# Which piece of SBUF comes next: slots of a backward pass chosen by megabytes stored since their return

## The chip, the core and the metric

The kernel runs on one core of one Trainium2 chip. The metric is the device time of one launch, in microseconds, as the median of several runs. One further execution is recorded by the hardware profiler, and its views are read below. Engine names are those of the profile: PE is the matrix engine, DVE the vector engine, ACT the scalar engine, POOL the GpSimd engine, SP the sync engine that here issues nearly all DMAs. MB are millions of bytes; a transfer that is called 1 MB or 2 MB in the code's terms has 1024 or 2048 KB.

## The reference

One decode step of an attention block with a cache and of a gated feed-forward block, forward and backward, in bfloat16. B = 4 rows, one query each, D = 512, H = 32 heads, a cache of Sk = 4096 positions, Dh = 128, F = 1792.

```python
q = (layernorm(x) @ wq) split into 32 heads            # [4, 32, 1, 128]
p = softmax(q . k_cache / sqrt(128))                   # k_cache, v_cache: [4, 32, 4096, 128]
h = x + (p . v_cache) @ wo
out = h + (silu(layernorm(h) @ w1) * (layernorm(h) @ w3)) @ w2
# outputs: out, and the gradients of sum(out * grad_out)
# for x, k_cache, v_cache, wq, wo, w1, w3, w2
```

With one query per head, the gradients of the two caches are outer products: for v_cache it is p (4096 long) times the gradient of the head's output (128 long), for k_cache it is the gradient of the scores times q. Each is as large as the cache itself. So the kernel must read both caches (2 x 134 MB), read v_cache once more in the backward pass for the gradient of p, and write two gradients of 134 MB each. The other gradients are small: out_4 (wq) and out_5 (wo) have 4.2 MB each, out_6, out_7, out_8 (w1, w3, w2) 1.8 MB each.

## The kernel before

The unit of work is one of 128 pairs (row, head), here called a head: 1 MB of k_cache and 1 MB of v_cache. The forward pass loads K and V of each head (lines 168 and 176 of the code). A middle part computes the feed-forward block and the gradients that lead to each head's output. The backward pass then goes over the heads again: the first SP = 32 one at a time (V loaded at L823, V gradient stored at L807, K gradient at L1234), the other 96 as NT = 48 pairs of heads. For a pair:

- `load_pair` (L1259) loads the two V of the pair with one 2 MB transfer,
- `front_pair` transposes them on PE (L1276), copies the result back over the same slots on ACT (L1277) and multiplies with dO, the gradient of the head's output (L1291); after that the V data are no longer needed,
- `grad_pair` takes two slots, fills them with an outer product on DVE (`outer_pair`, L1357) and stores them with one 2 MB transfer (L1367). It is called for out_3 (V gradient) by `more_V` and for out_2 (K gradient) in the loop over pairs.

DVE's outer products read p doubled by POOL (`P2_pair`, L1354, from rows that `P_rows` puts into the tile Pp by four matmuls and an ACT copy, L1329 and L1331) and rows of dO or q repeated over the partitions (`replicate_pair`, eight matmuls L1344 and an ACT cast L1347, once for four pairs and each of dO and q).

Beside the pairs runs `side_work`, a generator that is advanced by two yields at each call of `side`, four per pair. In this order it computes the gradient of x, the four 1 MB pieces of the gradient of wq (stored to out_4, L1057), loads w2 again (L528), makes row buffers rows1 and rows2 (a POOL DMA L1066, PE transposes L1074, ACT copies L1076), finishes the forward output (PE L1086, DVE L1091), and computes the gradients of w2 (L1101), w1 and w3 (L1117) and wo (L1128).

All data of this size live in one SBUF tensor, `arena`, of NSLOT = 23 slots of about 1 MB. `free` is a queue of free slots. A slot is returned to it in program order, at the moment the instructions that use it are written down, not when they are done: if its last use is a store, the next writer of the slot has to wait on the chip until the store has landed. Before the change a `Slot` takes the one that was returned first; names listed in `SIDE` take the first that lies outside `part["pairs"]`, the eight pairs of adjacent slots (0 to 5 and 8 to 17) that `Slot2` draws from, once `part["B"]` is set (from head 20 of the single heads on). `Slot2` takes the adjacent pair whose later half was returned first. So the lone slots are 6 and 18 to 22; slot 7 is in use throughout.

The order of all work is written out by hand in the loops, each engine executes its instructions in that order, and all large transfers go through SP's one queue, 530 of them. A transfer there also waits for the eighth one before it. Each is cut into sixteen parts, one per DMA engine, and each part leaves a record when it lands.

Of the kernel before, what the change touches and what calls it, by code (L numbers as in the profile page):

```python
# [18 lines left out]
NSLOT = 23  # L19
JQ = 8  # L20
NPE = 1
SP = 32
NPAIR = 8


@with_exitstack
def kernel(
# [25 lines left out]
    B = A_x.shape[0]  # L53
# [9 lines left out]
    DC = D // P  # L63
# [43 lines left out]

    free = deque(range(NSLOT))
    part = {"B": False, "side_done": False}
    SIDE = ("Pp", "wq2", "dqflat", "fin", "rows1", "rows2", "oflat", "w2a", "w2b", "gwq", "gw2", "gw13", "gwo")  # L110
    arena = slotp.tile([P, NSLOT * SLOT], BF16, name="arena")

    class Slot:
        def __init__(self, name, src=free):
            if name in SIDE and part["B"]:
                self.i = next(i for i in free if i not in part["pairs"])
                free.remove(self.i)
            else:
                self.i = src.popleft()
            self.t = arena[:, self.i * SLOT:(self.i + 1) * SLOT]  # L120

        def b(self, n=4096):
# [6 lines left out]
            return self.t[:, 0:SJ * Dh].rearrange("p (j d) -> p j d", d=Dh)  # L129

        def give(self):
            free.append(self.i)

    class Slot2:
        @staticmethod
        def choices():
            at = {i: n for n, i in enumerate(free)}
            return [(max(at[i], at[i + 1]), i) for i in (range(0, NSLOT - 1, 2) if part["side_done"] else sorted(part["pairs"])[::2])
                    if i in at and i + 1 in at]

        def __init__(self):
            self.i = min(self.choices())[1]
# [2 lines left out]
            self.t = arena[:, self.i * SLOT:(self.i + 2) * SLOT]  # L145

        def give(self):
            free.append(self.i)
            free.append(self.i + 1)


    rows_t = pers.tile([32 + B, D], FP32, name="rows_t")
# [45 lines left out]
    for i in range(2):  # L198
        t = fcon.tile([P, 64], BF16, name=f"onesw{i}")
# [132 lines left out]
    def zq_window(z, m):  # L332
        a = 66 * (m % 2) + 32 + (m % 2) - m
        return z[:, a:a + 32]
# [443 lines left out]
    REP = B  # L778
    reps = {}
    V2s, VTs = {}, {}  # L780
# [34 lines left out]
    NV2 = 7  # L815
    vring = deque()
    nv = {"next": 0}
# [137 lines left out]
    with ExitStack() as c2:  # L955
# [44 lines left out]
        def side_work():  # L1000
# [4 lines left out]
            t = rs.f(2080)[:, 1536:1536 + NH]  # L1005
# [6 lines left out]
            flat = Slot("dqflat")  # L1012
# [7 lines left out]
            for cc in range(DC):  # L1020
                wq2 = wq2s.popleft()
# [17 lines left out]
            fs = Slot("fin")  # L1039
# [10 lines left out]
            for cc in range(DC):  # L1050
                st = Slot("gwq")
                for n8 in range(HD // 512):
                    grad_unit(st.b(HD)[:, n8 * 512:(n8 + 1) * 512], xhat_bf[0:B, cc * P:(cc + 1) * P],
                              flat.b(HD)[0:B, n8 * 512:(n8 + 1) * 512])
                    yield
                grad_flush()
                nc.sync.dma_start(out=out_4[cc * P:(cc + 1) * P, :], in_=st.b(HD))  # L1057
                st.give()
            flat.give()
            fs.give()  # L1060
            w2 = load_w2()

            r1, r2 = Slot("rows1"), Slot("rows2")
# [40 lines left out]
            oflat = Slot("oflat")  # L1104
# [49 lines left out]
        def replicate(nm_, i0):  # L1154
            if i0 >= NH or (nm_, i0 // REP) in reps:
                return
            K_ = 8 * B if i0 < 8 * B else P
            rows = dOrows_bf if nm_ == "rdo" else qrows_bf
            ps = psrep.tile([P, REP, Dh], FP32, tag="rep", name="rep_ps")
            for i in range(REP):  # L1160
                nc.tensor.matmul(ps[:, i, :], lhsT=ident_b[0:K_, i0 + i:i0 + i + 1].to_broadcast([K_, P]), rhs=rows[0:K_, :],
                                 start=True, stop=True)
            rt = rep_bufs[nm_][i0 // REP % 2]
            nc.scalar.copy(out=rt, in_=ps[:])
            reps[nm_, i0 // REP] = rt
# [28 lines left out]
        def front(s):  # L1194
            hl = s % B
            if s not in VTs:
                for g in range(SJ // GW):
                    V_T(s, psT, range(g, g + 1))
                    if hl == 0 and g == 0:
                        rows_out()  # L1200
                    if hl == 0 and g == 2:
                        rows_T()
            VT = VTs[s].heads()
            if hl == 0:
                rows["acc"] = psD.tile([P, 512], FP32, tag="dP", name="dP_ps")
            dO_window(s + 2)
            for u in range(2):
                for c in range(4):
                    j0 = 8 * c + 4 * u
                    nc.tensor.matmul(rows["acc"][32 * c:32 * (c + 1), :], lhsT=zq_window(zd[hl], 2 * hl + u),  # L1210
                                     rhs=VT[:, j0:j0 + 4, :], start=(hl == 0 and u == 0),
                                     stop=(hl == B - 1 and u == 1), tile_position=(0, 32 * c))
            if hl == B - 1:
                rows["ps"] = rows.pop("acc")
            sl = VTs.pop(s)
            (vring if nv["next"] < SP and len(V2s) + len(VTs) + len(vring) < NV2 else free).append(sl.i)

        def group_dS(g):
            i0 = g * B
# [22 lines left out]
        NT = (NH - SP) // 2  # L1242
        H0 = SP // B
        pV, pP2, pdS, psl = {}, {}, {}, {}
        npv = {"next": 0}
# [13 lines left out]
            nc.sync.dma_start(out=pV[t].t[:, 0:2 * SJ * Dh], in_=two_heads(A_v_cache, t))  # L1259

        def load_pairs(t):
            while npv["next"] < NT and (npv["next"] <= t or len(V2s) + 2 * len(pV) < 6 and len(Slot2.choices()) > 1):
                load_pair()

        def dO_pair(t):
# [4 lines left out]
        def front_pair(t, mid):  # L1270
            pl = t % 2
            v = pV[t].t[:, 0:2 * SJ * Dh].rearrange("p (j d) -> p j d", d=Dh)
            for g in range(2 * SJ // GW):
                pt = psT.tile([P, GW, P], BF16, tag="tps", name="pt_tps")
                for i in range(GW):
                    nc.tensor.transpose(pt[:, i, :], v[:, g * GW + i, :], ident_b[:])  # L1276
                nc.scalar.copy(out=v[:, g * GW:(g + 1) * GW, :], in_=pt[:])  # L1277
                if pl == 0 and g == 0:
                    rows_out()
                if pl == 0 and g == 2:  # L1280
                    rows_T()
                if g == 3:
                    mid()
            if pl == 0:
                rows["acc"] = psD.tile([P, 512], FP32, tag="dP", name="dP_ps")
            dO_pair(t + 2)
            for u in range(4):
                m = 8 * pl + 2 * u
                for c in range(4):
                    j0 = 16 * c + 4 * u  # L1290
                    nc.tensor.matmul(rows["acc"][32 * c:32 * (c + 1), :], lhsT=zt[t % B][:, 32 - m:64 - m], rhs=v[:, j0:j0 + 4, :],  # L1291
                                     start=(pl == 0 and u == 0), stop=(pl == 1 and u == 3), tile_position=(0, 32 * c))
            if pl == 1:
                rows["ps"] = rows.pop("acc")
            pV.pop(t).give()

        def group_dS_pair(g):
            T = rows.pop("T").rearrange("p jj (c z l u a) -> p z l a c u jj", c=4, z=2, l=2, u=4, a=2)
# [11 lines left out]
        Pp, zt, P2b = {}, [], []  # L1310
# [23 lines left out]
        def replicate_pair(nm_, q):  # L1334
            if q >= NT // B or (nm_, "p", q) in reps:
                return
            s = SP + q * 2 * B
            K_ = 8 * B if s + 2 * B <= 8 * B else P
            rws = dOrows_bf if nm_ == "rdo" else qrows_bf
            ps = psrep.tile([P, REP, Dh], FP32, tag="rep", name="rep_ps")  # L1340
            for i in range(REP):
                for a in range(2):
                    n = s + i + a * B
                    nc.tensor.matmul(ps[64 * a:64 * (a + 1), i, :], lhsT=ident_b[0:K_, n:n + 1].to_broadcast([K_, P // 2]),  # L1344
                                     rhs=rws[0:K_, :], start=True, stop=True, tile_position=(0, 64 * a))
            rt = rep_bufs[nm_][(H0 + q) % 2]
            nc.scalar.copy(out=rt, in_=ps[:])  # L1347
            reps[nm_, "p", q] = rt
# [24 lines left out]
        def more_V(upto):  # L1373
            while gvd["n"] < min(SP, upto):
                s = gvd["n"]
                P_pairs(s)
                replicate("rdo", s - s % REP)
                grad_V(s)
                P_pairs(s + 1)
                P_pairs(s + 2)  # L1380
                gvd["n"] += 1
                if s % REP == 2 and s + 2 < SP:
                    replicate("rdo", s + 2)
                if s >= SP - 2:
                    P2_pair(s - SP + 2)
            while gvd["t"] < NT and SP + 2 * gvd["t"] + 2 <= upto:
                t = gvd["t"]
                P2_pair(t)
                replicate_pair("rdo", t // B)
                grad_pair(out_3, t, pP2.pop(t), reps["rdo", "p", t // B][:, t % B, :])  # L1390
                P2_pair(t + 1)
                gvd["t"] += 1
                if t % B == 2:
                    replicate_pair("rdo", t // B + 1)
# [57 lines left out]
        for t in range(NT):  # L1452
            s = SP + 2 * t
# [46 lines left out]
```

## Time and profile before

| | |
|---|---|
| median of 4 runs | 1697.9 us (1697.28 to 1698.45) |
| the profiled execution | 1698.45 us, of which the span of its instructions is 1696.7 us |
| bytes moved | 707.45 MB, mean 417 GB/s (read 422.59 MB, written 282.34 MB) |
| busy share of the span | PE 73%, DVE 73%, ACT 57%, POOL 20% |
| granted TensorE clock, mean | 0.857 |
| 2 MB stores (x96), issue to landing | 27.9 us |
| 2 MB V loads (x48), issue to landing | 32.1 us |
| where SP's queue waits longest in total | L1367 for DVE's outer products: 587.4 us in 94 waits |

The share of an engine is its busy time over the span. "DMA share" in a window is the mean busy share of the sixteen DMA engines, so one engine of sixteen that is busy alone gives 0.06. The number after an arrow in brackets is how long the engine was idle before the instruction, and on what it waited.

### The profile page before, as it was taken

What the parts mean: (1) busy time and instruction counts of PE and PEld (TensorE: products, weight loads), DVE (VectorE), ACT (ScalarE), POOL (GpSimd) and SP (SyncE); (2) the same over time, 40 slices, a digit from 0 to 9 for tenths busy, and PEclk for the clock granted to TensorE, in tenths of its full rate; (3) what the DMA queues carried; (4) which work ended last, traced back from release to release, by engine and by line L of the source; (5) the groups of instructions that cost most, each with busy time, mean ns of one, the idle gap of its engine ahead of it and who ended that gap; (6) DMA issues with size and microseconds to landing.
All of it is one profiled execution on the core that took longest, in us unless ns stands there. A gap on an engine that the chain in (4) does not pass through costs nothing. (4 is left out here: it accounts for less than half of the span.)

```text
span 1696.7 us, 37845 instructions
## 1 busy us (share of the span) xinstructions
PE 1237.8 (73%) x16228; PEld 950.2 (56%) x16228; DVE 1234.5 (73%) x1198; ACT 959.5 (57%) x1490; POOL 346.4 (20%) x583
## 2 busy tenths in 40 slices
PE   5889888888888888878877665666727766667552
PEld 4777766666677676656655544544425444444331
DVE  5989999999999987667764676575636665565582
ACT  3555454554455444677666566666628766566551
POOL 1211223222222222223331211021004100111000
PEclk9999999999999999799799679867659776676775
DMA  9999999999999999999999999999997999999997
GB/s 401 424 425 423 424 424 425 424 424 424 414 422 414 423 401 399 394 410 425 425 427 426 416 428 429 430 429 428 430 425 307 419 426 426 429 429 430 430 430 341
DMA packets 81000, 707.45 MB, mean 417 GB/s; under 512 B 8748, under 2 KB 12984, under 8 KB 15296
## 3 DMA queue, kind: packets, MB, share of 16 engines
q1 hardware_dynamic: 80416, 704.94, 99.0%
q8 instruction: 127, 2.08, 0.5%
q14 instruction: 41, 0.34, 0.0%
q0 software_dynamic: 416, 0.10, 0.0%
HBM read 422.59 MB, written 282.34 MB: 415 GB/s over the span
## 5 line engine op out<-in xcount | busy, mean ns | idle before, releaser
L1277 ACT COPY arena<-pt_tps 128x1024 bf16<-128x1024 bf16 x384 | 369.3, 1023 | 211.0 <-PE pt_tps L1276 210.6
L1276 PE MATMUL pt_tps<-ident_b,arena 128*128 128x128 bf16 x3072 | 307.0, 272 | 210.4 <-DMA arena<-in_A_v_cache_dram 128.4
L1276 PEld LDWEIGHTS <-arena 128*128 128x128 bf16 x3072 | 264.3, 126 | 311.5 <-issue 155.5
L1357 DVE TENSOR_TENSOR arena<-arena 128x8192 bf16<-128x8192 bf16 x48 | 212.3, 4424 | 255.9 <-DMA out_dram<-arena 224.1
L462 PE MATMUL M_ps<-arena 128*128 128x130 bf16 x4096 | 286.5, 222 | 38.3 <-DMA arena<-in_A_v_cache_dram 38.1
L447 DVE TENSOR_TENSOR arena<-arena 128x4096 bf16<-128x4096 bf16 x128 | 292.4, 2285 | 24.9 <-POOL arena L443 24.9
L462 PEld LDWEIGHTS <-arena 128*128 128x128 bf16 x4096 | 253.8, 99 | 58.9 <-DMA arena<-in_A_v_cache_dram 51.2
L354 DVE STREAM_TRANSPOSE arena<-arena 128x512 f32<-128x512 f32 (+1 forms) x321 | 250.6, 797 | 0.0
L349 ACT COPY arena<-pt_tps 128x1024 bf16<-128x1024 bf16 x128 | 129.4, 1012 | 186.7 <-PE pt_tps L348 147.7
L1357 DVE TENSOR_TENSOR arena<-dS,arena 128x8192 bf16<-128x8192 bf16 x48 | 212.3, 4425 | 19.8 <-DMA out_dram<-arena 19.6
L1354 POOL COPY arena<-arena 128x128 bf16<-128x128 bf16 x48 | 43.7, 911 | 496.7 <-ACT arena L1331 275.9
L360 POOL TENSOR_TENSOR W<-qrep,wmask 128x128 bf16<-128x128 bf16 x128 | 121.3, 948 | 84.9 <-PE S_ps L380 70.1
L791 ACT COPY arena<-pt_tps 128x1024 bf16<-128x1024 bf16 x128 | 122.1, 1024 | 29.0 <-PE pt_tps L790 27.1
L443 POOL COPY arena<-P_all 128x64 bf16<-128x64 bf16 x128 | 32.7, 255 | 413.5 <-ACT P_all L437 410.5
L790 PE MATMUL pt_tps<-ident_b,arena 128*128 128x128 bf16 x1024 | 83.4, 238 | 24.5 <-ACT arena L791 24.2
L790 PEld LDWEIGHTS <-arena 128*128 128x128 bf16 x1024 | 72.0, 109 | 35.2 <-issue 33.7
L1291 PE MATMUL dP_ps<-arena 128*32 128x512 bf16 x768 | 82.6, 454 | 10.4 <-ACT arena L1277 10.2
L796 DVE TENSOR_TENSOR arena<-P,arena 128x4096 bf16<-128x4096 bf16 x29 | 66.4, 2296 | 23.0 <-DMA out_dram<-arena 22.9
L437 ACT COPY P_all<-pt_P 32x64 bf16<-32x64 bf16 x256 | 52.1, 203 | 55.0 <-PE pt_P L433 52.7
L348 PE MATMUL pt_tps<-ident_b,arena 128*128 128x128 bf16 x1024 | 80.5, 223 | 0.0
L796 DVE TENSOR_TENSOR arena<-dS,arena 128x4096 bf16<-128x4096 bf16 x32 | 73.5, 2302 | 7.9 <-DMA out_dram<-arena 7.5
L472 PE MATMUL kP_ps<-arena,onesw 128*32 128x512 bf16 x1024 | 79.2, 386 | 0.0
(245 smaller groups left out, 1600.9 us busy)
## 6 DMA issues: line engine op xcount, KB each, us to landing
out_dram<-arena SPq DMA_DIRECT2D x96, 2048.0 KB, 27.9
arena<-in_A_v_cache_dram SPq DMA_DIRECT2D x160, 1024.0 KB, 15.8
arena<-in_A_k_cache_dram SPq DMA_DIRECT2D x128, 1024.0 KB, 15.4
arena<-in_A_v_cache_dram SPq DMA_DIRECT2D x48, 2048.0 KB, 32.1
out_dram<-arena SPq DMA_DIRECT2D x72, 1024.0 KB, 20.1
arena<-in_A_wq_dram SPq DMA_DIRECT2D x8, 1024.0 KB, 16.0
arena<-in_B_w_dram SPq DMA_DIRECT2D x8, 896.0 KB, 15.0
out_dram<-arena SPq DMA_DIRECT2D x6, 896.0 KB, 28.9
```

The lines of the kernel that those rows point to most:

```text
L349: nc.scalar.copy(out=KT[:, c * GW:(c + 1) * GW, :], in_=pt[:])
L354: nc.vector.transpose(out=KT[:, c * w_:(c + n) * w_], in_=Kn[:, c * w_:(c + n) * w_])
L360: nc.gpsimd.tensor_tensor(out=W[:, hl], in0=qrep[:, :, s:s + 1].to_broadcast([P, 4, 32]), in1=wmask[:, hl, None, :].to_broadcast([P, 4, 32 ...
L447: nc.vector.tensor_tensor(out=PK[:, :, 0:Dh].rearrange("p j (r t) -> p j r t", t=2), in0=Ks[s].heads().rearrange("p j (r t) -> p j r t", t=2),
L462: nc.tensor.matmul(hold["M"][:], lhsT=Vn[:, j, :], rhs=PK[:, j, :], start=(j == 0), stop=(j == SJ - 1))
L790: nc.tensor.transpose(pt[:, i, :], v[:, g * GW + i, :], ident_b[:])
L791: nc.scalar.copy(out=v[:, g * GW:(g + 1) * GW, :], in_=pt[:])
L796: nc.vector.tensor_tensor(out=dst.rearrange("p j (r t) -> p j r t", t=2), in0=col2[:, :, None, :].to_broadcast([P, SJ, Dh // 2, 2]), in1=r ...
L1276: nc.tensor.transpose(pt[:, i, :], v[:, g * GW + i, :], ident_b[:])
L1277: nc.scalar.copy(out=v[:, g * GW:(g + 1) * GW, :], in_=pt[:])
L1291: nc.tensor.matmul(rows["acc"][32 * c:32 * (c + 1), :], lhsT=zt[t % B][:, 32 - m:64 - m], rhs=v[:, j0:j0 + 4, :], start=(pl == 0 and u == ...
L1357: nc.vector.tensor_tensor(out=dst.rearrange("p (j r t) -> p j r t", r=Dh // 2, t=2), in0=col2[:, :, None, :].to_broadcast([P, 2 * SJ, Dh / ...
```

## The change

The slots of the backward pass are chosen by age instead of by their place in the queue. The age of a free slot is the number of slots with a store that were returned since its own return; a slot whose last use was not a store (a V slot after its transposes) counts as OLD = 9 at once. Side work takes the lone slot of greatest age. Other single slots take a lone slot if its age is 9 or more, else the oldest of all. `Slot2` takes the pair whose younger half is oldest. A V pair is loaded ahead only if the oldest free pair has an age of 9 or more. The two buffers flat and fs of the side work (slots of dqflat and fin) are returned just before the last slot of the wq gradient, not after it, and "lnb" becomes a name of the side work. The repeated dO rows of the first four pairs are made during head 30 of the single heads instead of at the first pair.

```diff
+OLD = 9
...
+    given = {"n": 0}
+
+    def age(i):
+        return given["n"] - given.get(i, -NSLOT)
+
+    def gave(*slots, stored=True):
+        given["n"] += len(slots) if stored else 0
+        for i in slots:
+            given[i] = given["n"] - (0 if stored else OLD)
+            free.append(i)
...
         def __init__(self, name, src=free):
-            if name in SIDE and part["B"]:
-                self.i = next(i for i in free if i not in part["pairs"])
-                free.remove(self.i)
-            else:
-                self.i = src.popleft()
+            self.i = src[0]
+            if part["B"] and src is free:
+                lone = sorted((i for i in free if i not in part["pairs"]), key=age, reverse=True)
+                self.i = lone[0] if name in SIDE or lone and age(lone[0]) >= OLD else max(free, key=age)
+            src.remove(self.i)
...
         def give(self):
-            free.append(self.i)
+            gave(self.i)
...
         def choices():
-            at = {i: n for n, i in enumerate(free)}
-            return [(max(at[i], at[i + 1]), i) for i in (range(0, NSLOT - 1, 2) if part["side_done"] else sorted(part["pairs"])[::2])
-                    if i in at and i + 1 in at]
+            return [(-min(age(i), age(i + 1)), i) for i in (range(0, NSLOT - 1, 2) if part["side_done"] else sorted(part["pairs"])[::2])
+                    if i in free and i + 1 in free]
...
                 nc.sync.dma_start(out=out_4[cc * P:(cc + 1) * P, :], in_=st.b(HD))
+                if cc == DC - 1:
+                    flat.give()
+                    fs.give()
                 st.give()
-            flat.give()
-            fs.give()
...
-            (vring if nv["next"] < SP and len(V2s) + len(VTs) + len(vring) < NV2 else free).append(sl.i)
+            if nv["next"] < SP and len(V2s) + len(VTs) + len(vring) < NV2:
+                vring.append(sl.i)
+            else:
+                gave(sl.i, stored=False)
...
-            while npv["next"] < NT and (npv["next"] <= t or len(V2s) + 2 * len(pV) < 6 and len(Slot2.choices()) > 1):
+            while npv["next"] < NT and (npv["next"] <= t or len(V2s) + 2 * len(pV) < 6 and len(Slot2.choices()) > 1
+                                          and -min(Slot2.choices())[0] >= OLD):
                 load_pair()
...
-            pV.pop(t).give()
+            gave(pV[t].i, pV.pop(t).i + 1, stored=False)
...
                 if s % REP == 2 and s + 2 < SP:
                     replicate("rdo", s + 2)
+                elif s % REP == 2:
+                    replicate_pair("rdo", 0)
```

The lists of instructions of POOL, SP and DVE keep their order, and no engine's list grows or shrinks. SP's 530 transfers keep order and size.

More of the change, by code (lines that the diff above doesn't have):

```diff
@@ L109 @@
     part = {"B": False, "side_done": False}
-    SIDE = ("Pp", "wq2", "dqflat", "fin", "rows1", "rows2", "oflat", "w2a", "w2b", "gwq", "gw2", "gw13", "gwo")
+    SIDE = ("Pp", "lnb", "wq2", "dqflat", "fin", "rows1", "rows2", "oflat", "w2a", "w2b", "gwq", "gw2", "gw13", "gwo")
     arena = slotp.tile([P, NSLOT * SLOT], BF16, name="arena")
+    given = {"n": 0}
[6 more added lines that the diff above has]
+            free.append(i)
     class Slot:
         def __init__(self, name, src=free):
-            if name in SIDE and part["B"]:
-                self.i = next(i for i in free if i not in part["pairs"])
-                free.remove(self.i)
-            else:
-                self.i = src.popleft()
+            self.i = src[0]
[3 more added lines that the diff above has]
+            src.remove(self.i)
             self.t = arena[:, self.i * SLOT:(self.i + 1) * SLOT]
@@ L147, in give @@
         def give(self):
-            free.append(self.i)
-            free.append(self.i + 1)
+            gave(self.i, self.i + 1)
     rows_t = pers.tile([32 + B, D], FP32, name="rows_t")
```

## Prediction

> **What bounds the kernel now.** I read the page first, then the waits, the timeline, the windows and the DMA issues, and last the trace's own records of DMA packets and landings.
>
> ```profile
> span 1696.7 us, 37845 instructions
> DMA  9999999999999999999999999999997999999997
> ```
>
> The DMA row is at 9 everywhere except slice 31 and the last one: 707.45 MB at a mean of 417 GB/s fill the span, and no compute engine is above 73%. Only two things can shorten this kernel: idle time of DMA engines, or fewer bytes. The change keeps all bytes, so I look for the idle time. Slice 31 lies at 1273 to 1315 us. The waits there:
>
> ```profile
> ACT arena L1076 <- DMA out_dram<-arena: 28.9, 1, 28.9
> POOL arena L1066 <- DMA out_dram<-arena: 55.2, 1, 55.2
> DVE arena L1357 <- POOL arena L1354: 19.9, 2, 19.6
> ```
>
> The timeline puts them in order:
>
> ```profile
> 1238.12 0.33 SPq L1057 DMA_DIRECT2D out_dram<-arena  x1
> 1254.77 0.34 SPq L1259 DMA_DIRECT2D arena<-in_A_v_cache_dram  x1
> 1267.01 0.90 ACT L1076 COPY arena<-pt_Tr 4x896 bf16<-4x896 bf16 x1 [28.92 <-DMA out_dram<-arena]
> 1269.10 4.42 DVE L1357 TENSOR_TENSOR arena<-arena 128x8192 bf16<-128x8192 bf16 x1 [19.61 <-POOL arena L1354]
> 1273.56 4.67 SPq L1367 DMA_DIRECT2D out_dram<-arena  x2
> 1278.33 0.51 SPq L1259 DMA_DIRECT2D arena<-in_A_v_cache_dram  x1
> 1299.29 0.33 SPq L1367 DMA_DIRECT2D out_dram<-arena  x1
> ```
>
> The last gwq store (to out_4) is issued at 1238.12. The row buffer rows1 gets that same slot, so ACT's first copy into it waits 28.92 us for the store to land. Behind that copy in ACT's order stand the copies of the next pair's transposes; DVE waits for POOL, POOL for ACT, and SP, which issues in order, sends nothing from 1254.77 to 1273.56 and nothing from 1278.33 to 1299.29. This is the hole:
>
> ```profile
> 1284.00:1288.00 4.00, 4.00 (x46) 2.53 (x45) 0.00 (x0) 2.88 (x4) 0.29 (x1) 0.71 0.94 381
> 1288.00:1292.00 4.00, 3.04 (x37) 2.15 (x36) 0.00 (x0) 3.79 (x6) 0.00 (x0) 1.00 0.54 225
> 1292.00:1296.00 4.00, 3.35 (x30) 1.76 (x28) 1.74 (x2) 1.47 (x3) 0.78 (x2) 1.00 0.07 29
> 1296.00:1300.00 4.00, 3.39 (x39) 1.68 (x38) 4.00 (x2) 2.97 (x4) 4.00 (x1) 1.00 0.07 28
> 1300.00:1304.00 4.00, 2.89 (x35) 2.19 (x33) 3.69 (x2) 3.82 (x6) 4.00 (x4) 1.00 1.08 455
> ```
>
> The last two columns are the DMA share and GB/s. The missing share is 4 × (0.06 + 0.46 + 0.93 + 0.93) = 9.5 us, and a dip at 1272 to 1276 adds 4 × 0.24 = 1.0: 10.5 us of idle transfer time. Read quickly, that is the gain.
>
> But the share falls to 0.07, not to 0. One engine of sixteen is 0.0625, and 28 GB/s is one sixteenth of the 428 to 430 GB/s at which all run. The packet records show packets back to back from 1290.96 to 1300.87, while the other fifteen engines start again at 1300.1 to 1300.3, after the store of 1299.29. **One DMA engine never stopped.** It had been behind. Each of SP's 530 transfers leaves sixteen landings; how far the last one is behind the median grows smoothly, 4.9 us at transfer 361 (914 us), 7.0 at 401, 9.6 at 421, 11.65 at 443, always a single straggler. After the hole it is 0.9 (transfer 447), and it grows again: 2.8 at 461, 5.1 at 501, 6.9 at 530, the last. So in the hole the fifteen waited for the one, and at the end the one lands at 1695.4 where the median is at 1688.5. The last windows show it:
>
> ```profile
> 1688.00:1692.00 4.00, 0.00 (x0) 0.00 (x0) 0.00 (x0) 0.00 (x0) 0.00 (x0) 0.50 0.25 107
> 1692.00:1696.00 4.00, 0.00 (x0) 0.00 (x0) 0.00 (x0) 0.00 (x0) 0.00 (x0) 0.50 0.05 20
> ```
>
> The end is thus set by an engine that had no idle time in the hole.
>
> **The change, part by part.** Instruction counts, SP's list of 530 DMAs and their sizes stay as they are; only slots change, and with them the waits.
>
> *The row buffers (the one part with a price).* rows1 moves to a slot last used by dqflat, rows2 to one of fin; neither was stored. ACT's 28.92 us and POOL's 55.16 us then go, and the chain of the hole with them. What I count is the slow engine's time from where the hole began. Transfer 443's last part lands at 1286.3; from there 171.2 MB remain. After the hole this engine ran from 1322.7 (transfer 450) to 1695.4 (530): 372.7 us for 156.5 MB, 2.382 us per MB. 171.2 × 2.382 = 407.8 us against the 409.1 us it took: -1.3. A dip at 1283 to 1285 in which it idled too adds -0.24. Sum -1.6 us (rounded up). The rate is the term that counts: 2.388 (transfers 369 to 443) makes it -0.3, 2.374 (451 to 530) -2.7, and 2.36 (470 to 530) -5.1. I take 2.382, the longest stretch after the hole.
>
> The Trainium skill ("DMA: Bandwidth & Descriptors", section "Latency and other measured facts") says that engines 7 and 15 are usually slower than the others in traces, with a cause it calls a guess. That speaks against a gain: a straggler that is a fixed engine keeps the end, and the sum stays near mine; were it chance, all 10.5 us would come back. No view here numbers the engines.
>
> *What is late next.* Without the stall, PE gets to the o2 product sooner, after eight side steps, two pair iterations of some 15 us, 30 us. w2's loads follow the out_4 store at 1238.5:
>
> ```profile
> arena<-in_B_w_dram SPq DMA_DIRECT2D x2, 896.0 KB, 30.8
> ```
>
> That median leaves a part or two on the slow engine some 33 us behind the issue, so PE waits 3 to 8 us. The cover: a 2 MB transfer takes 4.9 us, and out_3's store now often goes into the slots whose V load stands six DMAs earlier; 6 × 4.9 = 29 us, less eight ACT copies of 1.02 us and one gradient of 4.42 us on DVE, leaves 17 us of queued transfers. So 0 is taken; without the cover it would cost the 3 to 8 us, of which the slow engine, 11 us deeper in work than the rest, would still see nothing. The slot of the out_4 store passes to the first gw2 buffer, written eleven side steps (2.75 iterations, 41 us) after the issue; the landing took 28.9: 0, and 12 us in hand.
>
> *The other slots.* Before, the gradients of steady pairs reused a slot 11 MB after its store, V loads one some 24 MB after; now a gradient follows a store by 13 to 17 MB, or a load, and a V load follows a store by 14 to 16 MB. DVE's 243.7 us of waits for stores are idle time with full DMA queues beside it (share 1.0 outside the hole), so shortening them is worth 0. A V load waits at SP for a store seven or eight DMAs back, and SP already waits for the eighth to last: 0. The early waits of the new stage,
>
> ```profile
> SPq L1259 <- DMA out_dram<-arena: 17.3, 5, 7.2
> DVE arena L1357 <- ACT arena L1347: 11.9, 1, 11.9
> ```
>
> go or shrink: those loads now take slots 12 to 16 MB after a store instead of 5 to 10. The window 905 to 920 shows share 1.00 and 424 GB/s, so the worth is 0, at most -1.2 us, what the stretch 920 to 960 lacks against 428 GB/s.
>
> *dO rows sooner.* Eight matmuls (0.41 us) and a 0.59 us cast move ahead of four matmuls and a cast; DVE's 11.9 us wait shortens, the DMA share beside it is 1.01: 0, between +1.0 and -1.2.
>
> *Sum.* The profiled execution took 1698.45 us (span 1696.7 and 1.75 around it): 1698.45 - 1.6 = 1696.85. It is the highest of four with median 1697.9, so against the median: **1696.3 us**.
>
> **The rivals.** *The idle time does come back (faster).* If the straggler is not bound to one engine, or its lag stops growing, the median engine sets the end: it does 171.2 MB at 2.34 us in 400.6 us from 1274.6 (its landing of transfer 443), plus a lag that stays at 11.3: 1686.5 instead of 1695.4, -8.9. All sixteen: -10.5. That is 1687.4 to 1689.0; half the effect gives 1692.6. For it: a lag may have a ceiling, and the slow rate of the last transfers (2.36) is already better. Against: the lag grew without a bend from 4.9 to 11.65.
>
> *The stall moves to w2 (slower).* PE then waits at the o2 product for w2 and the transposes of the next pair stand behind it on PE, then ACT, DVE, SP, as in the hole. It decides from 17 us of waiting on (the cover above), and to be slower than before it must also use up the slow engine's depth. A wait like ACT's, 28.9 us, with the slow engine run dry too gives 28.9 - 17 = +12, less 1.6: 1708. Against it: w2's loads land some 31 us after an issue that PE is 30 us behind.
>
> *The change does not remove the wait* (the hole moves by some microseconds, to w2 or to the gw2 slot, at its old depth): 1697.9. It lies within my forecast's bounds.
>
> **How the numbers follow.** What a measurement of this kernel can tell from no change is about 0.2%, 3.4 us. My forecast (-0.3 to -2.7) and the unremoved wait lie within it, together 0.62. Faster: 0.29 (the idle time back, whole or half, and the 2.36 rate). Slower: 0.09, the moved stall and what it leaves of late transfers. The range: low 1687.5, which takes in the rival of the kept lag (1689.0) and most of the full one; high 1700.0, my forecast plus half of the 8 us wait at w2 uncovered. My case alone lies within 1694.5 to 1698.5.
>
> **What would show it.** Right: no ACT wait at the rows copy, no slice at 7 but the last, and last landings that reach some 18 us behind the median at the end (11.3 plus 6.9), so a longer tail with a DMA share near 0.06 and a median engine that ends about 9 us sooner. Wrong: a last landing less than 12 us behind the median with the time near 1688 (the first rival), or a PE wait of over 17 us for w2 with a DMA share of 0.07 or less around 1280 us (the second).

## The result: 0.15% slower, with the hole gone

| | before | after |
|---|---|---|
| median | 1698.38 us (61 runs, 1696.58 to 1701.0) | 1700.91 us (41 runs, 1699.13 to 1704.31) |
| ratio | | 1.0015, 95% interval 1.0011 to 1.002 |
| the profiled execution | 1698.45 us, span 1696.7 | 1699.13 us, span 1697.3 |

The profiled execution of after is the fastest of its 41, so its trace shows less than the 2.5 us of the medians. The head of its page, and two of its waits:

```profile
span 1697.3 us, 37873 instructions
DMA  9999999999999999999999999999999999999995
```

```profile
DVE arena L1372 <- PE dP_ps L1306: 238.8, 35, 15.1
DVE arena L1372 <- DMA out_dram<-arena: 4.1, 2, 3.8
```

The 7 in the DMA row is gone. The lines of the changed file stand 10 to 15 higher: L1372 is DVE's outer product (L1357 before), L1382 its store, L1306 the dP product of `front_pair`, L1273 the V pair load. Before, DVE waited 243.7 us for stores to land, as the same view of the kernel before says:

```profile
DVE arena L1357 <- DMA out_dram<-arena: 243.7, 74, 14.5
```

Now that is 4.1 us, and in its place stand 238.8 us of waits for PE. This is the new thing in the profile, and the timeline shows what it does:

```profile
985.00 0.45 SPq L1273 DMA_DIRECT2D arena<-in_A_v_cache_dram  x1
997.37 4.42 DVE L1372 TENSOR_TENSOR arena<-arena 128x8192 bf16<-128x8192 bf16 x1 [10.33 <-PE dP_ps L1306]
1001.82 0.33 SPq L1382 DMA_DIRECT2D out_dram<-arena  x1
```

SP issues a load at 985.00 and then nothing until 1001.82: DVE's gradient wants a pair of slots whose V data PE is still reading. The window (last two columns DMA share and GB/s) has the fifteen faster engines running dry:

```profile
1000.00:1004.00 4.00, 2.21 (x28) 1.85 (x28) 4.00 (x2) 4.00 (x6) 0.00 (x0) 1.00 0.83 348
```

Around the old hole, the timeline of after:

```profile
1236.60 0.89 ACT L1087 COPY arena<-pt_Tr 4x896 bf16<-4x896 bf16 x1
1240.59 1.15 SPq L1067 DMA_DIRECT2D out_dram<-arena  x1
1269.28 3.80 PE L1097 MATMUL o_ps<-arena 128*4 128x512 bf16 x14 [0.63 <-DMA arena<-in_B_w_dram]
```

ACT's first copy into the row buffer starts at 1236.60, with no wait, even before SP issues the last out_4 store; PE waits 0.63 us for w2. The tail has grown:

```profile
1660.00:1672.00 12.00, 6.11 (x60) 4.08 (x57) 4.34 (x7) 6.24 (x7) 0.00 (x0) 0.78 0.71 300
1688.00:1692.00 4.00, 0.00 (x0) 0.00 (x0) 0.00 (x0) 0.00 (x0) 0.00 (x0) 0.50 0.07 29
```

From 1660 on engines stand idle, and at 1688 to 1692 one is left (0.07) where before it was 0.25. The landing records say the same: transfer 443 of SP's list has its last part at 1286.3 us in both kernels, while the median part is at 1274.6 before and 1275.7 after. Before, the lag of the last part fell to 0.9 in the hole; after, it goes on to 13.5 at transfer 464 and 18.2 at 524. Then the fifteen idle: PE's transposes of the last V pair wait until 1656.73 for the load's last part, which the straggler brings, and store 529, which needs their result, is issued at 1674.15. Transfer 530 lands with 10.8 us of lag at 1696.0 (before: 1695.4). I call that straggler the slow engine.

### The profile page after: what moved, and what is told of

The parts are those of the page before. It is cut to its first block, busy times and chain, and to the rows that moved or that the text cites. A ratio compares the mean times of both kernels' runs of the same rounds, so it can differ in the third digit from the quotient of the medians.

```text
span 1697.3 us, 37873 instructions
## 1 busy us (share of the span) xinstructions
PE 1244.4 (73%) x16228; PEld 953.4 (56%) x16228; DVE 1232.0 (73%) x1198; ACT 959.4 (57%) x1490; POOL 357.3 (21%) x583
## 5 line engine op out<-in xcount | busy, mean ns | idle before, releaser
L1291 PE MATMUL pt_tps<-ident_b,arena 128*128 128x128 bf16 x3072 | 314.0, 276 | 200.9 <-DMA arena<-in_A_v_cache_dram 149.4
L1291 PEld LDWEIGHTS <-arena 128*128 128x128 bf16 x3072 | 269.9, 127 | 302.2 <-DMA arena<-in_A_v_cache_dram 175.7
L1372 DVE TENSOR_TENSOR arena<-dS,arena 128x8192 bf16<-128x8192 bf16 x48 | 213.0, 4440 | 182.0 <-PE dP_ps L1306 155.0
L1372 DVE TENSOR_TENSOR arena<-arena 128x8192 bf16<-128x8192 bf16 x48 | 212.2, 4422 | 98.1 <-PE dP_ps L1306 83.8
L1369 POOL COPY arena<-arena 128x128 bf16<-128x128 bf16 x48 | 72.0, 1501 | 433.9 <-ACT arena L1346 268.2
L801 ACT COPY arena<-pt_tps 128x1024 bf16<-128x1024 bf16 x128 | 121.8, 1025 | 29.5 <-PE pt_tps L800 26.8
L453 POOL COPY arena<-P_all 128x64 bf16<-128x64 bf16 x128 | 32.6, 255 | 412.7 <-ACT P_all L447 409.7
L800 PE MATMUL pt_tps<-ident_b,arena 128*128 128x128 bf16 x1024 | 81.3, 234 | 26.2 <-ACT arena L801 26.2
L1306 PE MATMUL dP_ps<-arena 128*32 128x512 bf16 x768 | 85.7, 486 | 7.3 <-ACT arena L1292 7.3
L358 PE MATMUL pt_tps<-ident_b,arena 128*128 128x128 bf16 x1024 | 80.5, 223 | 0.0
```

Of the source, the lines that this page charges most:

```text
L1372: nc.vector.tensor_tensor(out=dst.rearrange("p (j r t) -> p j r t", r=Dh // 2, t=2), in0=col2[:, :, None, :].to_broadcast([P, 2 * SJ, Dh / ...
```

## The experiments

The number I compare across traces is the time between the last landing of transfers 340 and 530, which is the slow engine's own time through the backward pass. A ratio is against runs of the kernel before on the same chip. The time comes from the one profiled execution and the ratio from all runs; the traces of the changed kernel are of executions below its median, so they show 1.6 us (after) and 1.1 us (after_again, 836.4) of its 2.5.

| kernel | ratio, 95% interval | slow engine 340 to 530, us | DVE's pair gradients wait for dP, us |
|---|---|---|---|
| before | 1 | 835.3 | none listed |
| rows_only | 0.9998 (0.9989 to 1.0007) | 835.3 | none listed |
| after_oldpairs | 0.9998 (0.9989 to 1.0007) | 835.1 | none listed |
| v_late | 0.9997 (0.9988 to 1.0006) | 835.3 | 40.5 |
| after | 1.0015 (1.0011 to 1.002) | 836.9 | 238.8 |
| after_no_dO | 1.0013 (1.0005 to 1.0022) | 837.5 | 212.8 |
| hole_back | 1.0019 (1.001 to 1.0028) | 838.1 | 204.7 |
| v_soon | 1.0031 (1.002 to 1.0043) | 841.1 | 269.9 |

### Is the hole worth anything?

In the expectations theory A is that of the prediction, one slow engine that sets the end; theory B has the end set by waits that the new slots bring.

rows_only changes the kernel before in one place:

```diff
-            flat.give()
-            fs.give()
             w2 = load_w2()
-            r1, r2 = Slot("rows1"), Slot("rows2")
+            r1, r2 = flat, fs
```

> The kernel before, with only rows1 and rows2 moved into the slots of flat and fs, which had no store; every other slot as before up to the end of the wq gradient. The wait of 28.9 us on ACT and the hole go. Theory A: last landings as in the kernel before to within 2 us, lag at the end about 18 us instead of 7, time within 2 us of before. Rival C (removing the hole itself costs, since the restart puts the sixteen engines in step): 2.5 us above before, like the changed kernel. Rival D (the hole is worth its 10 us, but the other slots of the change take it back): 8 to 10 us below before.

Measured: 1698.34 us against 1698.23. The hole is gone from its page,

```profile
DMA  9999999999999999999999999999999999999995
```

and what the fifteen engines gained in the middle they lose at the end (windows of the same kernel):

```profile
1660.00:1672.00 12.00, 5.10 (x52) 3.28 (x50) 5.06 (x6) 5.09 (x6) 0.00 (x0) 0.78 0.47 201
1688.00:1692.00 4.00, 0.00 (x0) 0.00 (x0) 0.00 (x0) 0.00 (x0) 0.00 (x0) 0.50 0.06 25
```

The slow engine's time is that of before, 835.3 us. Theory A holds, rivals C and D fall. hole_back asks the same from the other side:

```diff
                 self.i = lone[0] if name in SIDE or lone and age(lone[0]) >= OLD else max(free, key=age)
+                if name == "rows1":
+                    self.i = lone[-1]
```

> The changed kernel, but rows1 takes the slot of the last out_4 store again, so that ACT waits for its landing as before. Theory A: the hole of about 10 us is back in the DMA share near 1290 us, the lag at the end falls to about 7 us, and the time stays within 2 us of the changed kernel. Rival C: 2.5 us below the changed kernel. Rival D: 8 to 10 us above it.

Measured: 1701.89 us, ratio 1.0019, where the changed kernel has 1.0015 (their intervals overlap). The page shows the hole back:

```profile
DMA  9999999999999999999999999999979999999998
```

This hole is not a copy of the old one. It lies at 1260 to 1280, and at 1272 to 1276 the share is 0.04, less than one engine's 0.06: here the slow engine ran dry as well, and its transfers 442, 443 and 444 took 8.5, 6.2 and 6.3 us. The slow engine's time is 1.2 us over that of the changed kernel. So taking out a hole that left the slow engine busy was worth nothing, and putting in one that stopped it too cost about 1 us, which the intervals don't tell from 0. Something else in the change costs 0.15%.

### Taking work from the slow engine by cutting stores: a failure

after_spare and before_spare cut four stores:

```diff
-            nc.sync.dma_start(out=two_heads(out_ap, t), in_=g_.t[:, 0:2 * SJ * Dh])
+            dst, src = two_heads(out_ap, t), g_.t[:, 0:2 * SJ * Dh]
+            cuts = (0, 120, 128) if out_ap is out_2 and t in (8, 20, 32, 44) else (0, 128)
+            for p0, p1 in zip(cuts, cuts[1:]):
+                nc.sync.dma_start(out=dst[p0:p1], in_=src[p0:p1])
```

> The changed kernel, but four of the 48 out_2 pair stores (pairs 8, 20, 32, 44) are cut in two by rows: 120 of the 128 partitions in one transfer, 8 in a second one. Theory A (one of the sixteen DMA engines lags and sets the end): if the cut takes work from that engine, its lag behind the median, 18 us before the last stores, falls to a few us, the tail with a DMA share near 0.06 goes, and the time falls by 10 to 17 us (the median engine idles 7.4 + 10.8 us at the end now; equal shares give 15/16 of that). If the cut takes work from other engines, the lag grows and the time rises by up to 3 us. Theory B (the end is set by waits that the new slots bring): within 2 us of the changed kernel, with the lag changed or not.

> The kernel before with the same cut of four stores. Theory A: its engine lag at the end is only 7.2 us, because fifteen engines idled about 10 us around 1290 us; relieved of it, the kernel gains about 7 x 15/16 = 6.5 us, and it then stands 6 to 10 us above the changed kernel with the cut: the hole starts to cost once the slow engine is relieved. Theory B: within 2 us of the kernel before.

Measured: 1729.46 us (ratio 1.018, 1.0163 to 1.0196) and 1716.65 us (1.0114, 1.0099 to 1.0128). Both theories missed: a cut cost 4.6 us on average in the kernel before and 7.1 us in the changed one. In the trace of after_spare the packets between 1080 and 1120 us, around the first cut, took about 59 us longer in sum than is usual for their size, against about 4 us in the changed kernel. The lags were scattered afterwards: at transfer 412 of its list of 534 three engines were 5 to 6 us ahead of the median, two 6 to 7 us behind it and one 9.5 us. Which engine is the slow one can't be read from it, and whether the 120 rows or the 8 rows cost the time was not separated.

The Trainium skill ("DMA: Bandwidth & Descriptors", section "Why a DMA increments its semaphore by 16 and not by 1") says that a transfer from SP runs on the largest number up to 16 of engines that divides its rows, here 15 and 8, and that SP writes the rest of the count itself. The landing records agree: the cuts add 36 records, so a cut store leaves 25 instead of 16, which is 15 + 1 and 8 + 1.

### Which part costs it?

after_oldpairs puts the old rule back for pairs of slots alone:

```diff
-            return [(-min(age(i), age(i + 1)), i) for i in ...
+            at = {i: n for n, i in enumerate(free)}
+            return [(max(at[i], at[i + 1]), i) for i in ...
...
-                                          and -min(Slot2.choices())[0] >= OLD):
```

> The changed kernel with the old rule for pairs of slots (the pair returned first, no age, no limit on loading ahead); the row buffers, the single slots and the early dO rows stay as changed. The row buffers alone left the time of before unchanged (ratio 0.9998) and the hole put back left the changed kernel unchanged (1.0019), so the 2.5 to 3.7 us come from the rest. Theory P (the rotation of the pairs costs it): back to the kernel before within 1 us, and the long packets between 1000 and 1040 us (17.7 us in sum) go. Theory S (single slots or dO rows cost it): stays 2 to 4 us above before.

Measured: 1698.25 us against 1698.05, ratio 0.9998: the time of before. DVE waits for stores again,

```profile
DVE arena L1372 <- DMA out_dram<-arena: 266.2, 82, 11.3
```

and no window of 10 us from 900 to 1650 has a DMA share under 0.99, where after has 0.92 at 1000 to 1010. SP's transfers come in the same order in before, after and after_oldpairs, so the limit on loading ahead, which this edit also takes out, moved none of them: what differs is which slots they use. Theory P holds. after_no_dO takes the early dO rows out:

```diff
-                elif s % REP == 2:
-                    replicate_pair("rdo", 0)
```

> The changed kernel without the early dO rows of the first pairs: they are made at the first pair, as before. Theory P: unchanged, 2.5 us above before to within 1 us. Theory S, if the dO rows are its part: back to before within 1 us.

Measured: 1700.19 us against 1698.05, ratio 1.0013. The dO rows cost and bring nothing that can be seen.

> The changed kernel once more, for a second trace: the first was of an execution of 1699.1 us, 1.8 us below its median. The theory of one slow DMA engine expects the last landing of the 443rd transfer of SP's list at 1286 us again, and what is over the first trace's time as single long landings of that engine after it. If the extra time lies instead in waits of SP for slots, these grow.

Measured, the changed kernel once more: 1699.4 us in the one run, transfer 443 at 1286.7 us, and from there to the end 409.6 us against 409.7 in the first trace and 408.5 with the old pairs.

### Is it the wait for PE?

v_late and v_soon change how old a returned V pair counts at once, 4 or 20 in place of 9:

```diff
-            given[i] = given["n"] - (0 if stored else OLD)
+            given[i] = given["n"] - (0 if stored else 4)     # v_late; 20 in v_soon
```

> The changed kernel with one number changed: a V pair that comes back counts as 4 MB old at once, not 9. The old rule for pairs brought the time of before back (0.9998), so the rotation of the pairs costs the 2.5 us. In the changed kernel out_2's store takes the pair whose V was transposed in the same turn (loaded 8 to 10 transfers earlier), and DVE waits 238.8 us in 35 waits for PE's dP; with 4, gradients take V pairs loaded 11 to 13 transfers earlier, or stores 7 to 8 back. Theory W (these waits leave SP without work for up to 17 us, the fifteen engines run dry at 1000 and 1360 us, and the long packets that follow cost it): DVE's waits for dP nearly go, no dip at 1000 us, time within 1 us of before. Rival R (using all eight pairs for all purposes costs, whatever is waited for): stays 2 to 3 us above before.

> The same number at 20: a V pair that comes back is always the next one taken, by out_3's store, the first of the turn (7 to 9 transfers after its load). Theory W: DVE's waits for dP grow, more or longer dry stretches than in the changed kernel, 3 to 8 us above before. Rival R: as the changed kernel, 2.5 us above before to within 1 us.

Measured: v_late 1698.4 us against 1698.93, ratio 0.9997; v_soon 1703.51 us, ratio 1.0031. Their waits of DVE, v_late first, and then a window of v_soon:

```profile
DVE arena L1372 <- DMA out_dram<-arena: 197.2, 38, 10.6
DVE arena L1372 <- PE dP_ps L1306: 40.5, 17, 9.8
```

```profile
DVE arena L1372 <- PE dP_ps L1306: 269.9, 45, 11.3
```

```profile
1016.00:1024.00 8.00, 6.74 (x97) 4.86 (x97) 5.39 (x2) 6.81 (x8) 4.88 (x2) 1.00 0.56 236
```

v_late rotates all eight pairs for all purposes, as the changed kernel does, and has the time of before; rival R falls. The cost goes with DVE's waits for dP: 40.5 us of them cost nothing, 204.7 to 238.8 us (hole_back, after_no_dO, after) cost 0.13 to 0.19%, and 269.9 us, with a share of 0.56 over 8 us, cost 0.31%.

The number does more than the two expectations say. It also enters the limit on loading ahead, and the V loads of the first pairs move down SP's list by up to five places: in v_late up to transfer 393, in v_soon up to 383. From 394 on the order is the same in all these kernels, and there v_late still takes less than the changed kernel: 408.4 us against 409.7 from transfer 443 to the end. For v_soon the order is not separated: 2.8 us of what it takes over rows_only come between transfers 340 and 443.

How these waits become time of the slow engine is not shown. From transfer 443 to the end the three traces of the changed pairs without the hole (after, after_again, after_no_dO) take 409.7, 409.6 and 410.7 us, against 408.4 to 408.6 with rows_only, after_oldpairs and v_late (the kernel before, with its hole: 409.1). Loads 463 and 505 alone took the slow engine 5.33 and 5.09 us in after, 5.71 and 5.29 in after_again, 5.97 and 5.57 in after_no_dO, where the other three have 4.84 to 4.95. But load 463 took 5.97 us in the kernel before too. Load 463 lies in a stretch in which packets on many engines are long (41 us in sum at 1360 to 1440 in after, 4 us in rows_only). The dry stretch at 1360 that the expectation names shows in the second and third trace of the changed pairs (share 0.71 and 0.76 at 1364 to 1368); in the first the share there is 1.00. That dry stretches cause long packets was not tested, and neither decides by itself. v_late has a window with a share of 0.78 (1616 to 1620, where DVE had waited 10.51 us for a store), deeper than the 0.83 of the changed kernel at 1000, and long packets (17 us at 1480 to 1520), and loses nothing; after_oldpairs has no dry stretch and long packets all the same (24 us at 1600 to 1640).

### What slows the slow engine?

Between transfers 370 and 460 the slow engine takes 5.06 to 5.09 us for a 2 MB store and 4.85 for a load (medians of each trace), and in every trace its stores fall to about 4.85 after transfer 525, when PE and ACT have ended. Three kernels built on rows_only leave out work in pairs 24 to 47:

```diff
+            if t < 24:
                 outer_pair(...)                              # no_outer24
...
+                    if t < 24 or i == 0:
                         nc.tensor.transpose(...)             # no_trans24, no_tp24
-                nc.scalar.copy(out=v[:, g * GW:(g + 1) * GW, :], in_=pt[:])
+                w = GW if t < 24 else 1                      # no_trans24
+                nc.scalar.copy(out=v[:, g * GW:g * GW + w, :], in_=pt[:, 0:w, :])
```

> The kernel with only the row buffers moved (no hole), leaving out DVE's outer products of pairs 24 to 47: stores send what lies in the slots. It asks what slows the slow engine's stores (5.09 us for 2 MB against 4.85 for a load). Theory V (DVE's traffic in SBUF): from pair 24 on its stores take 4.86 us, its lag stops growing near 11 us, and the end comes 6 to 10 us sooner. Theory I (the work of PE and ACT, or the number of instructions): still 5.09 per store, lag and end as before to within 2 us.

> The kernel with only the row buffers moved, leaving out seven of eight of PE's transposes and of the elements of ACT's copies in pairs 24 to 47 (dP is then computed from the wrong layout). The slow engine's stores stayed at 5.07 us without DVE's outer products, and fall to 4.85 in every trace when PE and ACT end, near 1667 us. Theory I (PE's or ACT's work slows that engine): about 4.9 us per 2 MB store from pair 24 on, lag 3 to 5 us less at the end, end 3 to 5 us sooner than 1697.2. If neither: 5.07 and 1697 as before.

> As the run before it, but ACT still writes all elements, in eight small copies for each one left out: PE's transposes alone are cut to an eighth. If PE is what slows the engine: 4.9 us per store, as there. If ACT's work or number of instructions does: 5.07 or more.

Measured, one run each: no_outer24 1697.18 us (before: 1698.05), its stores between 485 and 521 5.08 us as in rows_only: theory V falls, and half of the pairs' DVE products gone move the end by under 1 us. no_trans24 1693.97 us and no_tp24 1693.07 us (before: 1698.93), stores 4.99 and 5.00 us, slow engine 831.0 and 830.9 us from 340 to 530. The 17 runs of the kernel before beside them begin at 1697.05. The groups of PE between 1500 and 1620 us, rows_only first, then no_trans24:

```profile
L1274 PE MATMUL pt_tps<-ident_b,arena 128*128 128x128 bf16 x468 | 50.7, 287 | 31.7 <-DMA arena<-in_A_v_cache_dram 24.4 <-ACT arena L1275 7.2
```

```profile
L1275 PE MATMUL pt_tps<-ident_b,arena 128*128 128x128 bf16 x58 | 12.6, 286 | 74.5 <-DMA arena<-in_A_v_cache_dram 70.5 <-ACT arena L1277 4.0
```

An eighth of the transposes, and the 48 stores of 2 MB between transfers 443 and 524 take 4.99 us in the mean instead of 5.07: 0.085 x 48 = 4.1 us, of 835.3 - 831.0 = 4.3 measured. ACT's copies, left out or kept in small pieces, make no difference. What gives the other 0.14 us over 4.85 was not found.

## Why the prediction was wrong

**The bound: right.** The end is set by one DMA engine that had no idle time in the hole. rows_only shows it by taking the hole away for nothing, and no_outer24 by its end: the median engine lands transfer 530 at 1675.2, the slow one at 1694.1. hole_back shows it less cleanly, since the slow engine idled there too. (A sixteenth of 428 to 430 GB/s is 26.8, not 28; the reading of one busy engine stands by the share and the landings.) "Only two things can shorten this kernel" left out a third, the pace of that engine: no_trans24 keeps all bytes and ends 4 to 5 us sooner.

**The row buffers: the wait and the hole went, and the size can't be told from 0.** Predicted -1.6 us (-0.3 to -2.7); rows_only, which is this part alone, gave 0.9998, that is -0.3 us with an interval from -1.9 to +1.2. In its trace the slow engine takes 408.6 us from transfer 443 on where it took 409.1, so -0.5. The rate was off: 408.6 us for 171.2 MB are 2.387 us per MB, the rate from before the hole (2.388). The 2.382 rests on 1322.7 us for transfer 450, whose last landing stands at 1324.0 in the trace. From there it is 371.4 us for 156.5 MB, 2.373, and the same sum would have given -2.8 in place of -1.3, further off.

**w2: right, and smaller.** PE waits 0.63 us for it where 3 to 8 were predicted. The gw2 buffer in the slot of the out_4 store shows no wait.

**The cover of 17 us, taken at 0: here it failed.** The working had the new dependence (a gradient takes the pair that a V load held shortly before) and the length of queue that it leaves, and used it only as cover for w2. It comes back at 35 gradients. The store of such a gradient stands mostly 8 to 10 transfers behind the load (30 of the 35), not six. But the load's last part comes with the slow engine, 4 to 18 us behind the median part, which the working left out, and the gradient starts 10 to 17 us after that, when the transposes and dP are done. DVE's wait reaches 15.1 us and SP's wait for DVE 17.5 us, as long as the 17 us of queued work. The window at 1000 us (share 0.83) is where it runs out; rows_only and after_oldpairs have no window of 4 us under 0.94 from 900 to 1650.

**"DVE's 243.7 us of waits for stores ... so shortening them is worth 0": the step's other half.** They were not shortened but exchanged, 243.7 us for stores against 238.8 us for dP. Waits for stores of 243.7 us (before), 266.2 (after_oldpairs) and 271.8 (rows_only) go with one time, and the exchange costs. The term was 0 and measured 2.5 to 2.9 us (the ratios 1.0013 of after_no_dO and 1.0015 of after, less 0.9998 of after_oldpairs). That the choice of pairs costs it is shown; by what path the waits reach the slow engine stays open.

**dO rows: 0, right** (1.0013 without, 1.0015 with).

**The signs to look for.** The lag of 18 us came (18.2), and the longer tail with one engine left. No slice stands at 7, and the last at 5. The median engine ended 3.3 us sooner (1685.2 against 1688.5), not 9. The working had left out that the last two stores hang on the last V load: its last part comes with the slow engine, then follow PE's transposes from 1656.73, dP, and DVE's product, and store 529 is issued at 1674.15, 6 us after the median landing of 528. So the fifteen wait there for the one.

**The rivals.** The idle time did not come back. The slower rival had the right kind of mechanism, DVE and SP behind a new wait for PE, but set it at w2, once and at +12 us; it happened at the pairs' slots, many times, and cost 2.5 us. The time, 1700.91, lies above the range, whose upper end held only half of a wait at w2. The rise of 2.5 us is less than the 3.4 us that the prediction took for the least that can be told from no change; 61 and 41 runs tell it (1.0011 to 1.002).

## What to carry to other kernels

When a change swaps a buffer that waits for a store against one that waits for a consumer, cost the new wait from the load's last landing through the consumer, at every turn of the loop, and compare it with the queue that is still in flight. Before counting idle DMA time as a gain, look whether the share falls to 0 or to one sixteenth: if one engine stays busy, the hole belongs to the others. None of the kernels here that do the whole computation beats the kernel before beyond its interval.

## What the runs showed of the hardware

- One DMA engine of sixteen lags in the mix of loads and stores: about 5.08 us for a 2 MB store where the median engine takes 4.87. It was slower while PE transposed (5.07 with 64 transposes per pair, 4.99 with 8, 4.85 with PE and ACT idle), and DVE's products made no difference.
- Cutting a 2 MB store of 128 rows into 120 and 8 cost 4.6 to 7.1 us on average, about as much as the transfer itself (4.87 us on the median engine).
